# Three early output stores split by rows: 112 rows over sixteen DMA engines, and twice 8 rows over the lowest eight

## The chip, the core and the metric

The kernel runs on one core of one Trainium2 chip. The metric is device time in microseconds (us) of one execution. A core has five instruction streams: TensorE (PE, with its weight loads shown apart as PEld), VectorE (DVE), ScalarE (ACT), GpSimd (POOL) and SyncE (SP). It also has sixteen DMA engines, which move everything between the chip's memory (HBM) and the on-chip buffer SBUF (128 partitions), whichever stream asks for it. A DMA is asked for in one instruction; it is then carried out as packets, here one packet for each partition's row.

## The reference

Four batches; q, k and v are 4 x 6400 x 256 in fp32, and the result is 25600 x 256 in fp32.

```python
qn = q / (norm(q, axis=1) + 1e-6);  kn = k / (norm(k, axis=1) + 1e-6)
s = kn.transpose(0, 2, 1) @ qn / tau            # 256 x 256 for each batch
a = softmax(s, axis=-1)
x = (v @ a).reshape(25600, 256)
logits = x @ w_gate                              # 8 experts, the best 2 are kept
w = softmax of the two kept logits
out = x + sum over the two experts e of  w_e * ((x @ A[e]) @ B[e])     # A: 256 x 16, B: 16 x 256
```

## The kernel before

The 6400 rows of a batch are laid out as 128 partitions of 50 chunks: partition p holds rows 50p to 50p+49. A chunk is thus 128 rows of 256 numbers. q and k of a batch come in three tiles of 17, 17 and 16 chunks (`QK`), v and the result in five tiles of 10 chunks (`V`, `PC`). All tiles of q, k and v are loaded by DMAs that POOL asks for (`do_load`, L561) and that turn fp32 into bf16 on the way; the first four chunks of q and k of batch 0 come as fp32 by SP and ACT. The result goes out in fp32 by DMAs that SP asks for (`do_store`, L926). A full store is one tile of 10 chunks: 128 rows of 10,240 bytes, 1,280 KB. The last two tiles of the last batch go out as three smaller stores each, of 4, 4 and 2 chunks (`FINE`, `UNITS`).

For a batch, the G steps (L587) multiply k by q over the 50 chunks into PSUM, and norms are taken beside it. Then a short chain of small steps (L648 to L765) makes the softmax and the small matrices for gate and experts. For each v tile then: transposes (L788), gate (L812, L826, L835), experts' inner product (L879), their transposes (L902), and the output matmuls Y (L915, L920), whose PSUM results ACT or DVE copies into a y tile (L769, L771). There are seven y tiles (`STORE["y"]`), so that finished results can wait in SBUF.

The order of all steps is fixed before the program is built: `make_plan` lists the steps with a cost, an engine and a rank, and `Plan.run` plays them through once as a simulated schedule. Each engine's instructions are then written out in that order. POOL asks for the loads in the order of `WORDS`, as far as tiles are free. SP carries the stores in the order of the plan. `HOLD` (L409) keeps some early stores back behind a named load: SP first asks for a 16-element DMA out of that load's last row into `scrap` (L645), which can only be asked for once the load has landed, and the stores queue behind it. In the order that SP has them, the first stores (batch, tile) are: (0,2); a hold on k (1,2); (0,1); (0,3); a hold on k (3,1); (0,0); (1,0); a hold on k (3,2); and then the rest, from (2,0) to (3,4). The constant tables `PARTS`, `FINE`, `FIRST`, `OFF` and `MERGED` (L413 to L423) hold other choices of the schedule.

The plan itself knows a store only as one step (`"store", b, i, c, n`) with a size; how many DMAs `do_store` asks for is not seen there.

Of the kernel before, what the change touches and what calls it, by code (L numbers as in the profile page):

```python
# [32 lines left out]
class Clock:  # L33


    WINDOW, FIRST, LOW, HIGH = 3.413, 0.31, 0.5, 0.8

# [3 lines left out]
    def at(self, t):  # L41
        w = max(0, int((t - self.FIRST) / self.WINDOW) + 1)
        while len(self.cold) <= w:
            share = self.busy[-1] / self.WINDOW
            self.cold.append(share < (self.HIGH if self.cold[-1] else self.LOW))
            self.busy.append(0.0)
        return w

    def took(self, t, us):

        end, w = t, self.at(t)
        while us > 1e-9:
            pace = 2.0 if self.cold[w] else 1.0
            step = min(us * pace, max(self.FIRST + w * self.WINDOW - end, 1e-6))
            self.busy[w] += step
# [5 lines left out]
    def idle(self, t):  # L61

        w = self.at(t)
        return t - self.FIRST - (w - 1) * self.WINDOW - self.busy[w] > self.SPARE

# [165 lines left out]
def make_plan(B, order, ahead):  # L231
# [150 lines left out]
    for b in range(B):  # L382
        for i in range(NP):
            x = pos["v", b, max(g for g, (i0, _) in enumerate(V) if i0 <= i)]
            parts = UNITS if b == B - 1 and i >= NP - FINE else ((0, PC),)
            for c, n in parts:
# [25 lines left out]

PARTS = {(0, 0): ((0, 2), (2, 15)), (0, 2): ((34, 8), (42, 8)), (3, 2): ((34, 8), (42, 8))}  # L413
FINE = 2
FIRST = 4
OFF = {(0, 0, 'k'), (0, 0, 'q'), (0, 1, 'q'), (0, 2, 'k'), (0, 2, 'q'), (0, 4, 'q'), (0, 5, 'q'),
        (0, 6, 'k'), (0, 6, 'q'), (0, 7, 'k'), (0, 8, 'q'), (1, 0, 'k'), (1, 0, 'q'), (1, 1, 'q'),
# [41 lines left out]
def kernel(  # L459
# [11 lines left out]
    nc = tc.nc  # L471

    B, N, C = q.shape
    P = 128
# [15 lines left out]
    out_v = out.rearrange("(b p c) d -> b p c d", b=B, p=P)  # L490
# [44 lines left out]
    held = {}  # L535
# [25 lines left out]
    def do_load(s, what, b, i, c, n):  # L561
        if what == "v":
            t, src, c0 = sb(s, "v", (b, i), [P, PC * max(n for _, n in V), C], BF16), v_v, c
        else:
            t = sb(s, "qk", (what, b, i), [P, max(n for _, n in QK), C], BF16)
            src, c0 = {"q": q_v, "k": k_v}[what], QK[i][0]
            if (b, c) == (0, 0):
                n = FIRST
                if "first" not in W:
# [6 lines left out]
        if (what, b, i) in (("q", 0, 0), ("k", 0, 0)):  # L576
            c, n = FIRST, c + n - FIRST
        nc.gpsimd.dma_start(t[:, c - c0:c - c0 + n, :], src[b, :, c:c + n, :])  # L578
# [346 lines left out]

    def do_store(s, b, i, c, n):  # L926
        lo = i * PC + c
        nc.sync.dma_start(out_v[b, :, lo:lo + n, :], held["y", (b, i), ""][:, c:c + n, :])


    do = dict(load=do_load, wts=do_wts, sq=do_sq, add=do_add, red=do_red, n2p=do_n2p, hold=do_hold, warm=do_warm, cast=do_cast, G=do_G, accs=do_accs, n2=do_n2, rsqrt=do_rsqrt, rq_ps=do_rq_ps, s=do_s,
              exp=do_exp, recip=do_recip, aT_ps=do_aT_ps, aT=do_aT, waA_ps=do_waA_ps, waA=do_waA,
              a=do_a, ZL=do_ZL, ZLe=do_ZLe, T=do_T, Te=do_Te, log=do_log, loge=do_loge, Z=do_Z, Ze=do_Ze, gzT=do_gzT,
              gzTe=do_gzTe, Y=do_Y, Ye=do_Ye, store=do_store)
    for name in ("m1", "eq1", "lm", "m2", "mask", "msum", "t", "th", "g2"):
        do[name] = gate_step(name)
# [50 lines left out]
```

## Time and profile before

| | us |
|---|---|
| median of 7 runs | 254.31 (254.15 to 254.48) |
| the profiled execution | 254.56 |
| its span, first to last instruction | 252.8 |
| PE / DVE / ACT / POOL busy in the span | 218.7 / 192.6 / 151.1 / 27.0 |
| first full store asked for | 76.72 |
| last store asked for | 247.5 |

The DMAs' part: 11,243 packets, 66.70 MB counted at the written side, 78.91 MB read from HBM and 26.21 MB written to it. The DMA queues are numbered: q0 carries what POOL asks for, q1 what SP asks for, q10 what ACT asks for, q8 and q14 the fetches of the engines' own instructions.

How it is read: a profile is one execution; busy time of an engine is the sum of its instructions, and a "share" of DMA is the time of the packets over sixteen engines times the span. The profile holds start, duration, queue and size of each DMA packet and, for each DMA, sixteen times at which a part of it landed. It does not hold the number of the DMA engine.

### The profile page before, as it was taken

What the parts mean: (1) busy time and instruction counts of PE and PEld (TensorE: products, weight loads), DVE (VectorE), ACT (ScalarE), POOL (GpSimd) and SP (SyncE); (2) the same over time, 40 slices, a digit from 0 to 9 for tenths busy, and PEclk for the clock granted to TensorE, in tenths of its full rate; (3) what the DMA queues carried; (4) which work ended last, traced back from release to release, by engine and by line L of the source; (5) the groups of instructions that cost most, each with busy time, mean ns of one, the idle gap of its engine ahead of it and who ended that gap; (6) DMA issues with size and microseconds to landing.
All of it is one profiled execution on the core that took longest, in us unless ns stands there. A gap on an engine that the chain in (4) does not pass through costs nothing.

```text
span 252.8 us, 5852 instructions
## 1 busy us (share of the span) xinstructions
PE 218.7 (87%) x2357; PEld 193.7 (77%) x2357; DVE 192.6 (76%) x528; ACT 151.1 (60%) x269; POOL 27.0 (11%) x54
## 2 busy tenths in 40 slices
PE   0274997988999998689999999889999979999990
PEld 0152983876999996579899899779999769999980
DVE  0055589879898987588899899489898898889840
ACT  5354437556786543975667768362674846657671
POOL 7003110040002002000500100500000000000000
PEclk9999897999999999999999999999999999999997
DMA  8999999999999999999999999999999999999996
GB/s 246 215 216 212 214 220 212 212 220 216 216 215 246 304 304 295 225 216 219 212 212 219 217 216 217 212 211 317 316 251 352 324 336 321 340 385 426 398 408 243
DMA packets 11243, 66.70 MB, mean 264 GB/s; under 512 B 1360, under 2 KB 1744, under 8 KB 6608
## 3 DMA queue, kind: packets, MB, share of 16 engines
q0 software_dynamic: 6912, 38.80, 74.4%
q1 hardware_dynamic: 3968, 26.87, 26.2%
q10 hardware_dynamic: 336, 0.66, 0.8%
q8 instruction: 18, 0.29, 0.4%
q14 instruction: 9, 0.07, 0.1%
HBM read 78.91 MB, written 26.21 MB: 416 GB/s over the span
## 4 chain that ended last, share of the span: by engine, by line
PE 53%; DMA 32%; issue 5%; DVE 4%; ACT 3%; POOL 1%; POOLq 0%; DVEq 0%
DMA v<-in_v_dram 18%; PE Y_ps L915 13%; PE acc L593 10%; DMA qk<-in_q_dram 10%; PE Y_ps L920 6%; PE T_ps L788 5%; PE ZL_ps L812 5%; DMA qk<-in_k_dram 5%; PE gzT_ps L902 4%; PE acc L597 3%; PE acc L602 2%; PE Z_ps L879 1%; ACT a_exp L715 1%; DVE a_bf L763 1%; PE log_ps L826 1%
## 5 line engine op out<-in xcount | busy, mean ns | idle before, releaser
L593 PE MATMUL acc<-qk 128*128 128x256 bf16 x400 | 69.4, 281 | 17.1 <-DMA qk<-in_k_dram 9.6
L915 PE MATMUL Y_ps<-a_bf,vT 128*128 128x256 bf16 x400 | 60.0, 272 | 0.2 <-DVE acc_sb L710 0.2
L621 DVE TENSOR_TENSOR ssq<-ssq,sq 128x1280 f32<-128x1280 f32 (+1 forms) x27 | 43.3, 1605 | 20.0 <-ACT sq L615 19.9
L769 ACT COPY y<-Y_ps 128x512 f32<-128x512 f32 x79 | 46.2, 586 | 16.5 <-PE Y_ps L920 13.5
L593 PEld LDWEIGHTS <-qk 128*128 128x128 bf16 x400 | 34.3, 101 | 20.3 <-DMA qk<-in_k_dram 11.0
L615 ACT ACTIVATE sq<-qk 128x1280 f32<-128x1280 bf16 (+1 forms) x27 | 36.9, 1367 | 17.7 <-DVE ssq L621 16.6
L915 PEld LDWEIGHTS <-vT 128*128 128x128 bf16 x400 | 39.0, 98 | 4.6 <-issue 0.3
L920 PE MATMUL Y_ps<-ball,gzT 128*128 128x256 bf16 x200 | 38.2, 273 | 0.0
L597 PE MATMUL acc<-qk 128*128 128x128 bf16 x242 | 34.4, 224 | 0.0
L788 PE MATMUL T_ps<-ident,v 128*128 128x128 f32 x200 | 27.5, 274 | 0.6 <-DVE waA_sb L757 0.4
L769 ACT COPY vT<-T_ps 128x512 f32<-128x512 f32 (+1 forms) x44 | 21.2, 510 | 11.1 <-PE T_ps L788 10.7
L597 PEld LDWEIGHTS <-qk 128*128 128x128 bf16 x242 | 24.3, 100 | 3.5
L890 DVE TENSOR_TENSOR gz<-zl,gateg 128x256 bf16<-128x256 f32 x70 | 26.3, 443 | 0.3
L578 POOL DMA_DIRECT2D v<-in_v_dram x20 | 11.5, 575 | 133.5 <-PE T_ps L788 119.7
L788 PEld LDWEIGHTS T_ps<-ident,v 128*128 128x128 f32 x200 | 22.3, 141 | 1.6 <-DVE waA_sb L757 0.6
L602 PE MATMUL acc<-qk 128*128 128x128 bf16 x168 | 23.4, 222 | 0.0
L902 PE MATMUL gzT_ps<-ident,gz 128*128 128x128 f32 x100 | 20.9, 281 | 2.6 <-DVE gateg L868 1.4
L920 PEld LDWEIGHTS <-gzT 128*128 128x128 bf16 x200 | 19.6, 98 | 2.3
L812 PE MATMUL ZL_ps<-waA_sb,vT 128*128 128x136 bf16 x280 | 19.5, 223 | 1.7 <-DVE waA_sb L757 1.5
L771 DVE COPY gzT<-gzT_ps 128x256 f32<-128x256 f32 (+1 forms) x40 | 15.0, 379 | 7.2 <-PE gzT_ps L902 5.6
L812 PEld LDWEIGHTS <-vT 128*128 128x128 bf16 x280 | 17.7, 98 | 2.4 <-issue 2.1
L615 ACT ACTIVATE ssq<-qk 128x1536 f32<-128x1536 bf16 x8 | 11.9, 1487 | 11.8 <-DMA qk<-in_q_dram 7.7
(80 smaller groups left out, 273.3 us busy)
## 6 DMA issues: line engine op xcount, KB each, us to landing
out_dram<-y SPq DMA_DIRECT2D x18, 1280.0 KB, 16.6
v<-in_v_dram POOLq DMA_DIRECT2D x20, 640.0 KB, 20.3
qk<-in_q_dram POOLq DMA_DIRECT2D x7, 1088.0 KB, 23.5
qk<-in_k_dram POOLq DMA_DIRECT2D x7, 1088.0 KB, 28.2
qk<-in_q_dram POOLq DMA_DIRECT2D x4, 512.0 KB, 19.4
qk<-in_k_dram POOLq DMA_DIRECT2D x4, 512.0 KB, 22.8
qk<-in_q_dram POOLq DMA_DIRECT2D x2, 1024.0 KB, 19.4
qk<-in_k_dram POOLq DMA_DIRECT2D x2, 1024.0 KB, 23.7
```

What stands on the lines that cost most here:

```text
L593: nc.tensor.matmul(acc[ic][:, 0:256], kt[:, j, ic::CC], qt[:, j, :], start=c == 0, stop=False, skip_group_check=True)
L597: nc.tensor.matmul(acc[ic][:, 256:384], kt[:, j, ic::CC], kt[:, j, ic::CC], start=False, stop=False, skip_group_check=True)
L602: nc.tensor.matmul(acc[ic][:, 384:512], qt[:, j, ic * P:(ic + 1) * P], qt[:, j, ic * P:(ic + 1) * P], start=False, stop=c == NC - 1, skip_ ...
L615: nc.scalar.activation(out[:, 0:n, :], t[:, j:j + n, :], ACT.Square)
L621: nc.vector.tensor_tensor(out=t, in0=t, in1=held["sq", (w, b, g), ""][:, 0:n, :], op=OP.add)
L769: nc.scalar.copy(out, in_)
L788: nc.tensor.matmul(ps[:, j, :], vt[:, c + j, :].bitcast(FP32), W["ident32"], is_transpose=True, start=(j == 0), stop=(j == n - 1))
L812: nc.tensor.matmul(ps[:, j, :], vT_of(b, i, c + j)[:, :, ic], st[b]["waA"][:, ic, :], start=(j == 0 and ic == 0), stop=(j == n - 1 and ic ...
L890: nc.vector.tensor_tensor(out=pairs[:, h].rearrange("p c (e r) -> p c e r", e=E), in0=z[:, 2 * h:2 * h + 2, :].rearrange("p c (e r) -> p c ...
L902: nc.tensor.matmul(ps[:, j, :], pairs[:, j * P:(j + 1) * P], W["ident32"], is_transpose=True, start=(j == 0), stop=(j == n // 2 - 1))
L915: nc.tensor.matmul(ps[:, j, :], vT_of(b, i, c + j)[:, :, ic], st[b]["a"][:, ic, :], start=(j == 0 and ic == 0), stop=False, skip_group_che ...
L920: nc.tensor.matmul(ps[:, j, :], pair[:, :, j], W["B"], start=False, stop=(j == 1), skip_group_check=True)
```

## The change

`do_store` looks the tile (batch, tile) up in a new table, `SPLIT`. For three tiles, (0,2), (0,3) and (0,0), it asks for three DMAs in place of one: partitions 0 to 111, then 112 to 119, then 120 to 127, all with the same columns. The other stores are asked for as before, as one DMA of 128 partitions. The plan, the order of the steps, the loads and the computation stay as they are.

```diff
 FINE = 2
+SPLIT = {(0, 2): ((0, 112), (112, 8), (120, 8)), (0, 3): ((0, 112), (112, 8), (120, 8)), (0, 0): ((0, 112), (112, 8), (120, 8))}
 FIRST = 4
...
     def do_store(s, b, i, c, n):
         lo = i * PC + c
-        nc.sync.dma_start(out_v[b, :, lo:lo + n, :], held["y", (b, i), ""][:, c:c + n, :])
+        for p, rows in SPLIT.get((b, i), ((0, P),)):
+            nc.sync.dma_start(out_v[b, p:p + rows, lo:lo + n, :], held["y", (b, i), ""][p:p + rows, c:c + n, :])
```

A DMA of 112 rows is divided over sixteen engines as seven rows each, and one of 8 rows over the lowest-numbered eight engines as one row each. For the three tiles together, the lowest eight engines so carry 27 rows each in place of 24, and the highest eight 21.

## The prediction

> **What bounds the kernel now.** I began with the head of the page, because a change to stores can only matter where DMA does.
>
> ```profile
> span 252.8 us, 5852 instructions
> PE 218.7 (87%) x2357; PEld 193.7 (77%) x2357; DVE 192.6 (76%) x528; ACT 151.1 (60%) x269; POOL 27.0 (11%) x54
> DMA  8999999999999999999999999999999999999996
> q0 software_dynamic: 6912, 38.80, 74.4%
> q1 hardware_dynamic: 3968, 26.87, 26.2%
> q10 hardware_dynamic: 336, 0.66, 0.8%
> q8 instruction: 18, 0.29, 0.4%
> q14 instruction: 9, 0.07, 0.1%
> ```
>
> PE is busy for 87%, but the DMA row has a 9 in every slice but the first and the last, and the shares of the queues add up to 74.4 + 26.2 + 0.8 + 0.4 + 0.1 = 101.9% of sixteen engines' span (a packet starts some ns before the one ahead of it ends, so over 100 is possible). The second view, busy time by stretches, shows where there is room at all. Its columns are the stretch, its length, busy time of PE, PEld, DVE, ACT and POOL, granted clock, DMA share, GB/s.
>
> ```profile
> 106.00:166.00 60.00, 57.82 (x629) 52.74 (x627) 51.28 (x134) 40.97 (x74) 8.46 (x16) 1.00 1.04 215
> 226.00:238.00 12.00, 12.00 (x150) 11.32 (x149) 10.98 (x37) 8.18 (x19) 0.00 (x0) 1.00 1.01 423
> 238.00:240.00 2.00, 2.00 (x26) 1.89 (x25) 1.65 (x5) 0.93 (x4) 0.00 (x0) 1.00 0.83 342
> 240.00:248.00 8.00, 6.83 (x61) 5.79 (x59) 3.26 (x10) 5.92 (x11) 0.00 (x0) 1.00 1.00 407
> 248.00:252.80 4.80, 0.00 (x0) 0.00 (x0) 0.00 (x0) 0.00 (x0) 0.00 (x0) 0.65 0.48 191
> ```
>
> The DMA engines are full until 238, some of them rest between 238 and 240, and after 248 only DMAs run. So an engine's end is the sum of its own packets, and the kernel's end is that of the slowest engine. The chain of waits names PE for 53%, as it runs back from the last store through the matmuls. But the last store is asked for at 247.47, its first part lands at 249.98, and its last at 252.05: the end is decided by those 2.07 us between DMA engines.
>
> The third view is the trace's packets and landings. All rows are dealt evenly, so why do engines differ? The sixteen landings of a store in the stretch of stores (asked for at 219.65) and of the last store:
>
> ```
> 219.65: 232.81 232.91 233.06 233.07 233.56 233.59 233.89 | 235.01 235.08 235.20 235.30 235.31 235.41 235.53 235.72 236.53
> 247.47: 249.98 249.99 250.01 250.03 250.06 250.15 250.23 | 250.51 250.64 250.74 250.84 250.97 251.16 251.17 251.88 252.05
> ```
>
> Seven engines are early and nine late. A packet follows the one before it on its engine at a fixed offset, so I chained the packets into sixteen tracks by their ends and by the order that each queue gives an engine. (Where two tracks pass within some ns they can be exchanged; I know of such places near 170 and 240.) The 18 q8 packets, 16 KB of instructions each, take 0.95 us on average (17.1 in all), and the engine that has one falls back by that much. They go to only eight tracks, in a fixed rotation: 30.6, 48.8, 59.1, 72.1, 84.1, 94.0, 111.9, 122.4, and again in that order from 134.0 and from 226.8. So two engines carry three blocks and six carry two. These eight are among the late nine, and the two with three are those that land last. The ninth late track holds five q14 packets (8 KB, 0.31 to 0.32 us and slower neighbours; 50.6, 103.5, 157.9, 201.7, 246.0). These come at the pace of DVE's instructions. I put its last landing at 251.16.
>
> The Trainium skill ("Runtime: NRT & Kernel Launch", Instruction fetch mechanics) says that instructions stream in blocks of 16 KiB and that crossing a boundary is mostly hidden. The size agrees; hidden it is for PE, but not for the DMA engine, which is held for 0.95 us. By the rule alone all engines would end together, and moving rows to eight of them could only delay the end.
>
> **The change part by part.**
>
> *Rows moved.* A 10,240-byte packet of a store takes 0.394 us from start to next start beside loads, and 0.381 when only stores run. The three stores lie beside loads. Each of the lowest eight engines gets 27 rows for 24: +3 x 0.394 = +1.18 us. Each of the highest eight gets 21: -1.18. Neither is lost on the way, as no engine rests before 238.
>
> *Extra ends.* Each DMA ends with a packet of 4 bytes on each engine it uses, some 0.01 us: six more on the lowest eight, +0.06.
>
> *Extra issues.* SP issues six more DMAs at 0.333 to 0.366 us each.
>
> ```profile
> 76.72 0.37 SPq L928 DMA_DIRECT2D out_dram<-y  x1
> 77.83 0.60 SPq L645 DMA_DIRECT2D scrap<-qk  x1
> 78.48 0.56 SPq L928 DMA_DIRECT2D out_dram<-y  x1
> 89.82 0.33 SPq L928 DMA_DIRECT2D out_dram<-y  x1
> 166.95 0.51 SPq L645 DMA_DIRECT2D scrap<-qk  x1
> 167.51 1.05 SPq L928 DMA_DIRECT2D out_dram<-y  x2
> ```
>
> Behind (0,2) at 76.72 the hold is queued. It goes out at 77.83, after its load has landed at 77.81; 0.37 + 2 x 0.33 us puts SP at 77.75, still before it. Behind (0,3) at 89.82 nothing is issued until 166.95. Behind (0,0) stands (1,0), 0.67 us later, but its packets wait in the ring for some 6 us behind those of (0,0) anyway. So nothing; without this cover it would be 0.67 us at one place. The y tiles come free after three landings in place of one; the last of them is up to 1.2 us later on a lowest engine. Seven tiles cover this. If they did not, PE would lose 1.2 us at most, and PE has the 2.5 us from the last issue to the first landing behind a DMA end that is later still.
>
> *The price of a row in the new form.* The trace has no store of 8 or 112 rows. Below, a row costs what it costs now (0.394). Above, the nearest row is a store packet just behind an instruction block, which reads up to 0.767, +0.37. As for many engines on few partitions, in the first us sixteen engines write 512-byte rows into 32 partitions and hold 0.027 us a packet until 4.7; later they slow to 0.05, together with the other queue's packets. That row is the nearest in kind, and up to 4.7 it shows no toll. I take 0 and keep up to +0.37 for each of the six single rows (2.2 us on the lowest eight).
>
> The Trainium skill speaks against the new form: "SBUF — State Buffer" (Door 1: The DMA port swizzle) has 112 to 127 on four of sixteen ports, and "DMA: Bandwidth & Descriptors" (Rules for kernel authors) advises one transfer of 128 partitions over two for halves. By it, four engines reading one port would take 4 x 0.385 = 1.54 us where each row now takes 0.385. No run here shows it.
>
> *The sum.* What matters is which tracks are the lowest eight; the trace gives no numbers. If the eight with the blocks are the upper half, the two worst go from 252.05 and 251.88 to 250.87 and 250.70, a relief of 1.18. But the lower half then holds the seven early tracks and the ninth late one. The early ones have 1.1 us of rest at 238 to 240 and 1.8 us at the end, so +1.24 costs nothing there. The ninth goes from 251.16 to 251.16 + 1.24 = 252.40: it becomes the last, and the end moves by 252.40 - 252.05 = +0.35. On the profiled 254.56 that is 254.91; the profiled execution is 0.25 above the median, so on the median it is 254.66, and as the late tracks beside the ninth end a little earlier, I say 254.6. Three rows are more than the balance asks for: with one row the last would be 251.66.
>
> **The rivals.**
>
> *A, above: traded.* The relieved eight give up 1.18, the engine of DVE's instructions takes over: 254.6. If its track is taken wrongly by one place (neighbours 250.5 to 251.17), the end lies between 251.75 and 252.41, thus 254.0 to 254.7; with some toll 254.9.
>
> *B, the wrong half.* If the blocks go to the lowest eight, or to a mix that holds one with three, that one gets all: 252.05 + 1.24, +1.24 us: 255.55. It decides as soon as one of the two three-block tracks has a number below eight. For it: nothing in the trace ties a rotation of eight to the upper half. Against it: nothing either. Where a store or load meets empty rings, block tracks start 0.1 us later on average in the four loads after 191, which would suit higher numbers, but the spread of single starts is 0.4 or more.
>
> *C, the toll.* Single rows out of 8 neighbouring partitions, or seven rows out of blocks not aligned as before, are slower. With half of the bound, 6 x 0.185 = 1.1 on the lowest eight, and 0.02 for each of the 21 other rows, 0.4: +0.35 + 1.5, about 256.1. It decides from a toll of 0.03 us a single row on, the point at which 254.8 is passed. Against it stand the 512-byte rows, for it that all 128-row stores share rows out in one way, and these not.
>
> *D, relief that lasts.* If the ninth late track is not among the lowest eight, the end falls to the next of the late ones: 252.05 - 1.18 = 250.87, -1.18, or some of that: 253.6 as a middle. Against it: eight block tracks leave no room in the upper half for a ninth.
>
> *E, not as said.* If the 8 rows go to other engines each time, or to sixteen, the shift is spread thin, and 254.3 stays.
>
> **How the numbers follow.** Chances: A 0.43, B 0.22, C 0.17, D 0.12, E 0.06. A measurement of this kernel can tell about 0.2% from no change, 0.5 us. Below 253.8: most of D, and a little of A for a track taken wrongly, 0.13. Between 253.8 and 254.8: A's larger part, E, the rest of D, 0.43. Above 254.8: B, C, and 0.05 of A, 0.44. The likeliest is A at 254.6, within 254.0 to 254.9 for itself. The range is 253.6 (the middle of D) to 256.1 (the middle of C); it leaves out half of D and half of C.
>
> **What would show it.** Right: the sixteen landings of the last store no longer fall into seven and nine with two stragglers; the two three-block tracks end 1.2 us earlier against the early seven, and one track with 8 KB blocks ends last, near 252.4; store packets of 10,240 bytes keep 0.39 us; SP's hold still goes out at 77.8. B is right if the three-block tracks lie 1.2 us further out. C shows in store packets of 0.5 us and more between 80 and 105. D shows in a last landing below 251.7. Wrong altogether would be a DMA row with slices under 9, an end that follows PE's last matmul, or a shift of the tail by something other than some multiple of a row's 0.39 us.

## The result, and the profile after

| | before | with the change |
|---|---|---|
| median (range), us | 254.35 (254.15 to 254.54) | 255.34 (254.73 to 255.91) |
| ratio | | 1.0039, 95% interval 1.0031 to 1.0047 |
| profiled execution, its span | 254.56, 252.8 | 255.13, 253.3 |
| last store asked for, last landing | 247.47, 252.05 | 247.13, 252.47 |
| span's end minus last landing (span not rounded) | 0.74 | 0.84 |

The change costs 0.99 us (0.79 to 1.20); the forecast was 254.6, +0.3, so its sign was right and its size a third. The range of single runs is three times as wide as before, 1.18 us against 0.39.

The head of the page of the changed kernel:

```profile
span 253.3 us, 5864 instructions
PE 219.5 (87%) x2357; PEld 194.0 (77%) x2357; DVE 192.7 (76%) x528; ACT 151.2 (60%) x269; POOL 27.0 (11%) x54
DMA  8999999999999999999999999999999999999995
q0 software_dynamic: 6912, 38.80, 74.2%
q1 hardware_dynamic: 4016, 26.87, 26.2%
q10 hardware_dynamic: 336, 0.66, 0.8%
q8 instruction: 18, 0.29, 0.4%
q14 instruction: 9, 0.07, 0.1%
```

Bytes, shares and busy times are those of before; only q1 has 4016 packets for 3968, the 48 extra ends (six DMAs of 8 rows, eight engines each), which is what the edit says. The busy time by stretches (stretch, length, busy time of PE, PEld, DVE, ACT and POOL, granted clock, DMA share, GB/s):

```profile
106.00:166.00 60.00, 57.83 (x630) 52.76 (x627) 51.28 (x134) 40.80 (x74) 8.46 (x16) 1.00 1.03 215
238.00:240.00 2.00, 2.00 (x27) 1.86 (x25) 2.00 (x6) 0.93 (x3) 0.00 (x0) 1.00 0.90 374
240.00:248.00 8.00, 6.48 (x58) 5.46 (x56) 2.91 (x9) 5.57 (x11) 0.00 (x0) 1.00 1.00 411
248.00:253.30 5.30, 0.00 (x0) 0.00 (x0) 0.00 (x0) 0.00 (x0) 0.00 (x0) 0.66 0.42 169
```

Between 238 and 240 the engines are busy for 0.90 in place of 0.83. That does not show that rows have filled the early tracks' rest: the kernel before with two small DMAs, in which no row moves (below), has 0.93 there. After 248 still only DMAs run, so it is still the slowest DMA engine that ends the kernel. SP's queue in order of time (start, length, instruction, count):

```profile
76.94 1.08 SPq L930 DMA_DIRECT2D out_dram<-y  x3
78.12 0.59 SPq L646 DMA_DIRECT2D scrap<-qk  x1
167.55 0.52 SPq L646 DMA_DIRECT2D scrap<-qk  x1
168.11 1.78 SPq L930 DMA_DIRECT2D out_dram<-y  x4
```

The three issues of (0,2) take 1.08 us, and the hold goes out at 78.12. Its load landed at 77.83 in this execution, 0.29 us earlier; in the kernel before, the hold followed its load by 0.02 (77.83 and 77.81). The next load's hold, at 167.55, stands 0.6 behind that of before, and no slice of the DMA row falls below 9 for it. The landings of the last store:

```
before   249.98 249.99 250.01 250.03 250.06 250.15 250.23 250.51 250.64 250.74 250.84 250.97 251.16 251.17 251.88 252.05
after    249.68 249.69 249.71 249.72 249.76 249.80 250.02 250.10 250.65 250.93 251.03 251.07 251.12 251.81 251.82 252.47
```

I chained the packets into sixteen tracks again; now the 8-row DMAs name the half of each track, and the first two split stores give their single rows to the same eight tracks. Between the halves, these two stores make a difference of 1.58 us = 4 x 0.394 (two rows more on one side, two fewer on the other). The track with DVE's 8 KB blocks is among the lowest eight and ends last, at 252.47. Of PE's eight block tracks, six are in the upper half, the two with three blocks among them; the third and the fourth of the rotation (blocks at 60.1 and 72.0) are in the lower half, and end at 251.81 and 251.82. Of the 48 single-row packets 44 take 385 to 398 ns; four are slow, in two pairs that overlap in time: 668 and 888 ns at 87.2, 1086 and 752 ns at 177.8 and 178.05. Overlap alone does not make a row slow: of the first 8-row DMA, seven single rows run at one moment (starts 85.76 to 86.12) at 385 to 398 ns each.

### The profile page after: what moved, and what is told of

The parts are those of the page before. It is cut to its first block, busy times and chain, and to the rows that moved or that the text cites. A ratio compares the mean times of both kernels' runs of the same rounds, so it can differ in the third digit from the quotient of the medians.

```text
span 253.3 us, 5864 instructions
## 1 busy us (share of the span) xinstructions
PE 219.5 (87%) x2357; PEld 194.0 (77%) x2357; DVE 192.7 (76%) x528; ACT 151.2 (60%) x269; POOL 27.0 (11%) x54
## 3 DMA queue, kind: packets, MB, share of 16 engines
q1 hardware_dynamic: 4016, 26.87, 26.2%
## 4 chain that ended last, share of the span: by engine, by line
PE 45%; DMA 40%; issue 6%; DVE 3%; ACT 2%; POOL 1%; POOLq 0%; DVEq 0%
DMA v<-in_v_dram 18%; DMA qk<-in_k_dram 13%; PE Y_ps L916 12%; DMA qk<-in_q_dram 9%; PE acc L594 7%; PE Y_ps L921 6%; PE T_ps L789 5%; PE ZL_ps L813 4%; PE gzT_ps L903 4%; PE acc L598 2%; PE acc L603 1%; PE Z_ps L880 1%; POOL qk L579 1%; ACT a_exp L716 1%; PE log_ps L827 1%
```

## The experiments

Theory A is the balance of rows: an end is worth 0.394 us times the rows moved, and DVE's track takes over. The rivals are a toll on rows in the new form, and, after the first four kernels, a third thing that was not on my list: the end of the program. All times are medians in us; each set of kernels ran beside the kernel before, which is 254.35 to 254.43 in every set, and kernels of different sets are compared through it. The landings and the last column come from one profiled execution of each kernel.

| kernel | DMAs more | median (range) | ratio to before, 95% interval | last landing | from there to the span's end |
|---|---|---|---|---|---|
| one split | 2 | 254.50 (254.30 to 255.08) | 1.0006, 0.9997 to 1.0015 | 251.63 | 1.09 |
| two splits | 4 | 254.74 (254.55 to 255.09) | 1.0016, 1.0007 to 1.0025 | 251.80 | 0.97 |
| 16 rows in place of 8 + 8 | 3 | 254.70 (254.56 to 254.83) | 1.0012, 1.0003 to 1.0021 | 251.92 | 1.04 |
| six splits | 12 | 257.40 (256.89 to 257.63) | 1.0116, 1.0102 to 1.0130 | 254.20 | 0.96 |
| one split, six small DMAs | 8 | 254.03 (253.95 to 254.63) | 0.9990, 0.9981 to 0.9998 | 251.43 | 0.72 |
| before, two small DMAs | 2 | 254.77 (254.57 to 255.10) | 1.0016, 1.0007 to 1.0025 | 251.80 | 1.10 |
| the change, two small DMAs | 8 | 255.18 (254.71 to 255.61) | 1.0038, 1.0025 to 1.0052 | 252.20 | 0.74 |
| extra rows, neighbours | 6 | 256.30 (256.20 to 256.47) | 1.0078, 1.0065 to 1.0090 | 253.84 | 0.84 |
| extra rows, spread | 6 | 256.27 (256.03 to 257.13) | 1.0083, 1.0067 to 1.0098 | 253.36 | 0.86 |
| the change again | 6 | 255.06 (254.95 to 255.82) | 1.0034, 1.0022 to 1.0047 | 252.64 | 0.84 |
| five DMAs, neighbours | 16 | 255.46 (255.36 to 256.07) | 1.0044, 1.0030 to 1.0057 | 253.53 | 0.74 |
| five DMAs, spread | 16 | 254.85 (254.71 to 255.40) | 1.0018, 1.0009 to 1.0026 | 252.16 | 0.73 |

### How many rows

One split store, (0,2) alone:

```diff
-SPLIT = {(0, 2): ..., (0, 3): ..., (0, 0): ...}
+SPLIT = {(0, 2): ((0, 112), (112, 8), (120, 8))}
```

> Only the store (0,2) is split. Balance of rows (each split gives the lowest eight engines one row more, +0.41 us with its ends, and takes 0.39 us from the upper eight; nothing else): the two tracks with three 16 KB blocks go from 252.05 to 251.66, the track with DVE's instruction blocks from 251.16 to 251.57, so the end moves by -0.39 us: about 253.95 us. Toll (single rows out of eight neighbouring partitions are held up, which made the difference between 0.35 and the measured 0.99 us with three splits, so 0.2 us a split): about 254.15 us, with one or two single rows of 0.6 us or more between 86 and 89.

Two, (0,2) and (0,3):

> The stores (0,2) and (0,3) are split, (0,0) is not. Balance of rows: DVE's track ends at 251.16 + 0.82 = 251.98, the three-block tracks at 251.26: -0.07 us, 254.3 us, no change that can be told. Toll of 0.2 us a split on top of it: 254.7 us. If the time is as with three splits, the third split costs nothing and the reason lies in the first two.

Six, (0,1), (1,0) and (2,0) beside the three:

> The first six stores are split, (0,2), (0,1), (0,3), (0,0), (1,0), (2,0). Balance of rows: DVE's track takes six rows, 251.16 + 6 x 0.41 = 253.62: +1.57 us, 255.9 us. Toll of 0.2 us a split beside it: another 1.2 us, 257.1 us. If early engines' rest near 239 could take the rows in, the time would stay near that of three splits.

With one row moved the last landing is at 251.63, where the balance had 251.66, and yet the kernel is not faster: 254.50, above both expectations (253.95 and 254.15), with no slow single row in its profile. With two it is 251.80 (balance 251.98), and the kernel is 0.38 slower; that is the time that the toll was expected to give, but this profile has no slow single row either. So the landings follow the balance, and the time does not follow the landings. With six the last landing is 0.6 past the balance, and store packets are slow: between 193.9 and 198.7 twenty of them take 0.65 us or more, the worst 1527 ns. The last split store, (2,0), has only sixteen single rows, so ordinary rows are among these. The DMA row of that page shows for the first time a slice under 9 between the first and the last (near 240):

```profile
span 255.2 us, 5873 instructions
DMA  8999999999999999999999999999999999999894
```

### The form without the rows

```diff
+SPLIT = {x: ((0, 112), (112, 16)) for x in ((0, 2), (0, 3), (0, 0))}
```

> The same three stores as 112 rows and one DMA of 16 rows, which goes to all sixteen engines: every engine keeps its 24 rows, and nothing is moved between them. Balance of rows: only three ends of 0.01 us are added: 254.4 us, no change. Toll: 16 single rows a store instead of 16 on eight engines, so as many single rows in all, now on the late tracks of the upper half as well: 0.3 to 0.9 us, 254.7 to 255.3 us, with single rows of 0.6 us or more. If the form with 112 rows alone costs time (engines no longer read the same partitions as before), it shows here too, in packets of the 112 rows.

The last 16 rows of the same tiles go to sixteen engines, one row each, so nothing moves between halves. None of the 48 single rows is slow and the last landing, 251.92, is 0.13 earlier than in the profile before; the kernel is 0.34 slower all the same. Neither a toll nor the balance explains that; what is left is the time after the last landing, 1.04 us in place of 0.74.

### The end of the program

The trace has SP's waits at the very end, after its last store: one instruction for each pair of semaphores, in a fixed order of numbers. Each DMA of SP and ACT is given one of eight semaphores in turn. From the records of SP (start of the instruction, the DMA semaphore that it waits for, and the last landing of that kernel):

```
before      111 at 248.98   116 at 250.22   117 at 251.43   118 at 252.07                     (landing 252.05)
one split   107 at 251.02   108 at 251.64   109 at 251.71   110 at 251.77   111 at 251.83
            116 at 251.89   117 at 251.95   118 at 252.01                                     (landing 251.63)
```

Before, SP and ACT ask for 32 DMAs, four full turns, so the last store is on 118, which is waited for last: 0.02 us after the landing this wait is over, and only the program's last few instructions follow. With two more, the last store is on 108, and six waits of 0.06 us still follow, though all they wait for has landed: +0.37. With three it is five waits, with four or twelve it is four, with six (the change) two, +0.12. The time from the last landing to the end goes in these steps in all fourteen profiles: 0.72 to 0.74 with no wait behind, 0.84 to 0.86 with two, 0.96 to 0.97 with four, 1.04 with five, 1.09 to 1.10 with six. To test it, small DMAs of 4 bytes, asked for while SP is idle near the start, turn the semaphores on:

```diff
+        for x in range(6):
+            nc.sync.dma_start(pad[:, x:x + 1], moe_w_gate[0:1, x:x + 1])
...
+    pad = nc.dram_tensor("pad_words", (1, 8), FP32, kind="Internal").ap()
```

> One split store (0,2), and six DMAs of 4 bytes each at the start (from HBM to a spare tensor in HBM), so that the number of DMAs of SP and ACT grows by eight, one full rotation of the eight semaphores, in place of two. Theory 'balance and end waits': the last landing stays at 251.6 to 251.8 as with one split alone, the last store is again on the semaphore that SP waits for last, and the 0.37 us of six more waits are gone: 0.75 us from last landing to end of span in place of 1.07, median 254.0 (253.9 to 254.15). Rival 'the end waits cost nothing' (the last landing is not what ends the kernel): 254.5 as with one split alone.

> No split at all; two DMAs of 4 bytes at the start, from HBM to a spare tensor in HBM. No row of a store moves and no form of a store changes. Theory 'end waits': the last store goes to the second of the eight semaphores that SP waits for at the end, six more waits of 0.06 us follow the last landing: +0.37 us, 254.7 (254.6 to 254.8), with the last landing still at 252.05. Rival 'the end waits cost nothing': 254.35.

> The change whole, and two DMAs of 4 bytes at the start (from HBM to a spare tensor in HBM): eight more DMAs than before, so the last store is on the last semaphore again. Theory 'balance and end waits': last landing 252.4 to 252.6, tail 0.75, so 0.12 us less than the change alone: 255.2. Theory 'toll by chance': single-row packets of over 0.6 us again, at other places and in another number than in the profile of the change (4 of 48), and the range of the runs over 0.8 us wide; median 255.0 to 255.4. Rival 'toll by place': the same two pairs are slow, near 87 and 178.

All three times came out as the end waits have it; the last landings came out 0.17 to 0.25 earlier than expected. The kernel before, with two such DMAs and nothing else, is 0.39 slower (254.77; from its last landing to the end 1.10 in place of 0.74). One split with a full turn is 254.03, 0.47 under the same split without it. Its page and its issues of SP (the second fence: what is written, how many, KB each):

```profile
span 252.2 us, 5863 instructions
DMA  8999999999999999999999999999999999999996
q1 hardware_dynamic: 3996, 26.87, 26.2%
```

```profile
out_dram<-y SPq DMA_DIRECT2D x2, 80.0 KB
pad_words<-in_moe_w_gate_dram SPq DMA_DIRECT2D x6, 0.0 KB
```

In packets the six DMAs cost twelve of 4 bytes (3996 = 3968 + 16 ends + 12 of the small DMAs), and the span is 0.5 us shorter than with one split alone (252.7). This is the one version that is faster than the kernel before, by 0.35 us between the medians; the ratio's interval, 0.9981 to 0.9998, stops just short of 1. The kernel before with eight small DMAs, a full turn without any split, was not run. The change itself with a full turn is 255.18, 0.16 less than without, which is within the width of its runs. Its slow single rows came back near 178 (702, 1012 and 753 ns), not near 87.

### The price of a row

Six extra rows on the lowest eight engines, taken off no one, from neighbouring partitions or from partitions that lie 16 apart:

```diff
+        for x in range(2 if (b, i) in SPLIT else 0):
+            nc.sync.dma_start(spare[SPLIT.index((b, i)), x], held["y", (b, i), ""][slice(112 + 8 * x, 120 + 8 * x), c:c + n, :])
```

and for the spread copy `slice(7 + 8 * x, P, 16)`.

> All stores as before, and behind each of the stores (0,2), (0,3) and (0,0) two more DMAs of 8 rows each, from partitions 112 to 119 and 120 to 127, into a spare tensor in HBM (extra work, no part of the result). The lowest eight engines get six rows more, the upper eight give none up; six more DMAs, so the end waits are those of the change. Theory 'balance': the lowest engine with a late track goes from 251.16 by 6 x 0.394 + 0.06 to 253.6; span 254.4, 256.1 us median (255.8 to 256.4), and the copy with spread partitions the same. Theory 'toll by neighbouring partitions': single-row packets of 0.6 us and more here, 256.5 and over, and over 0.3 us more than the copy with spread partitions.

> The same as the copy with neighbouring partitions, but the two more DMAs of 8 rows take partitions 7, 23, 39 ... 119 and 15, 31, 47 ... 127, so that the eight rows of one DMA lie 16 partitions apart. Theory 'balance': 256.1 us (255.8 to 256.4), as with neighbours. Theory 'toll by neighbouring partitions': no single-row packet over 0.5 us, 256.1, while the copy with neighbours is over 0.3 us slower. Theory 'toll of the single row as such' (a DMA with one row an engine, wherever it lies): slow single packets here too, and no difference between the two copies.

> The change once more, word for word, for a second profile and a second set of runs beside the copies. Theory 'toll by place': single-row packets of (0,0) near 177.8 are slow a third time (752 to 1086 ns so far); those near 87 may be or not. Theory 'toll by chance': slow ones elsewhere or none. Median 255.2 to 255.5 by both, range over 0.8 us wide.

Both copies are at 256.3, 0.2 above the balance's 256.1: the arithmetic of rows holds over six rows as it did over one. The copy with neighbours has two slow single rows (972 and 871 ns at 179.7), the spread one has none; the medians show no difference. The change run again is at 255.06, below the 255.2 to 255.5 expected, with slow rows at 86.5 (1095 and 569 ns) and again near 179 (621, 1035 and 741 ns). So slow rows stand near 178 in all three profiles of the change, and near 87 in two of them.

That left open whether slow rows cost the change anything, so the last pair puts the question to the change's own rows. Each of the three stores goes out as five DMAs, 64, 32, 16, 8 and 8 rows; in one copy the partitions of a DMA are neighbours, in the other they lie 2, 4, 8 and 16 apart. Sixteen more DMAs (four of them small) make two full turns.

```diff
+ROWS = (slice(0, 128, 2), slice(1, 128, 4), slice(3, 128, 8), slice(7, 128, 16), slice(15, 128, 16))
+SPLIT = {(0, 2): ROWS, (0, 3): ROWS, (0, 0): ROWS}
...
-        nc.sync.dma_start(out_v[b, :, lo:lo + n, :], held["y", (b, i), ""][:, c:c + n, :])
+        for r in SPLIT.get((b, i), (slice(0, P),)):
+            nc.sync.dma_start(out_v[b, r, lo:lo + n, :], held["y", (b, i), ""][r, c:c + n, :])
```

The copy with neighbours has `slice(0, 64), slice(64, 96), slice(96, 112), slice(112, 120), slice(120, 128)`.

> The same three stores, each as five DMAs of neighbouring partitions: 64, 32 and 16 rows (four, two and one row on each of sixteen engines), and twice 8 rows as in the change. The same rows move to the lowest eight as in the change. With four DMAs of 4 bytes at the start there are sixteen more DMAs than before, two full rotations, so the tail after the last landing is 0.75 us. Theory 'balance': as the change with two such DMAs, 255.2, and 0.1 for the extra ends: 255.3 (255.0 to 255.5). Theory 'toll of neighbouring partitions': slow single-row packets (over 0.6 us) here, more than the four or so in the change, as sixteen rows more are single: 255.4 to 255.9.

> The same as the copy with neighbouring partitions, but the five DMAs take every second partition, then every fourth, eighth and twice every sixteenth of the rest: the rows that engines read at one time lie apart. Theory 'balance': 255.3, no difference between the two copies. Theory 'toll of neighbouring partitions': no slow single rows, a narrow range of the runs, and 0.2 to 0.5 us under the copy: 254.9 to 255.0, which is what the balance alone gives from the landings of an undisturbed kernel before (DVE's track at 251.2 + 1.24 = 252.44 against 251.8: +0.64 on 254.35).

255.46 against 254.85: rows that lie apart save 0.61 us, and the two intervals (1.0030 to 1.0057 and 1.0009 to 1.0026) do not meet. All five DMAs are spread in that copy, not the single rows alone. With neighbours two single rows are slow, 981 ns at 178.3 and 1180 ns at 178.8, fewer than expected; with spread rows none is, but the range of its runs is no narrower (0.69 us against 0.71). The last stretch of the two (neighbours first):

```profile
248.00:254.30 6.30, 0.00 (x0) 0.00 (x0) 0.00 (x0) 0.00 (x0) 0.00 (x0) 0.50 0.33 134
```

```profile
248.00:252.90 4.90, 0.00 (x0) 0.00 (x0) 0.00 (x0) 0.00 (x0) 0.00 (x0) 0.56 0.41 162
```

Both have nearly the same work left at 248: 6.30 x 0.33 = 2.08 and 4.90 x 0.41 = 2.01 us an engine, alike within the rounding of the shares. Yet the first ends 1.4 us later: its landings are all in by 251.88 but for one, at 253.53. So the delay sits on one engine. The slow packets explain only part of it: they overlap in time, so they lie on two engines, and one engine lost at most 0.79 us (1180 over 394 ns). The profiles also show the extremes: of the neighbours one of the two slowest of five runs (256.07), of the spread rows the fastest of eleven (254.71).

## Why the prediction was right and wrong

**The bound: right.** DMA stays full to 238, nothing but DMA runs after 248, and the last landing moves with the rows: 251.63, 251.80, 252.47 and 254.20 for one, two, three and six. (Without a split it was 252.05 in one execution and 251.80 in another, so 0.2 between two of them tells little.)

**Rows moved, 3 x 0.394: right.** 1.58 between the halves after two stores; one row gave 251.63 for 251.66, six extra rows 256.3 for 256.1.

**Who is last: right, with one detail wrong.** "If the eight with the blocks are the upper half" holds for six of the eight. The two that are not did not matter: they had two blocks, and end 0.65 before DVE's track. Case A names the track and its end, 252.40 for 252.47. The nearest to a case where only rows decide is the spread copy with five DMAs: +0.42 (254.85 - 254.43), for +0.35 predicted. One small step in that sum was loose: I took the 0.25 by which the profiled execution lies above the median off all tracks alike. In the kernel before with two small DMAs the last three landings are 251.20, 251.79 and 251.80, so in that execution the surplus is gone from the three-block tracks alone, and the sum on the median would have been 251.20 + 1.24 - 251.80 = +0.64. The 0.42 lies between the two.

**The toll, taken as 0: the step that failed.** I let the 512-byte rows at 0.027 us stand for it, because they were the nearest in kind. They are small loads into 32 partitions, and say nothing about rows of 10 KB read out of 8. The pair of five DMAs puts a price on neighbouring partitions, 0.61 with 96 single rows; the change has 48. (The extra copies, with 48 single rows, put it at nothing: 256.30 and 256.27.) For the change itself the toll is only what is left over: 0.99 - 0.12 - 0.42 leaves 0.45, the change with a full turn of semaphores 255.18 - 254.38 - 0.42 some 0.4, the second set of runs 255.06 - 254.35 - 0.12 - 0.42 leaves 0.2. With 0.64 for the balance in place of 0.42 it would be 0.2 or nothing, so its size stays open. Case C had the toll, but in another form: not 0.03 us or more on every row, but three to five rows in 48 that lose 0.2 to 0.7 us each. Such a row can cost the kernel only where it falls on an engine that ends late; whether that made the range of the runs wide is not shown, as kernels without slow rows in their profile have wide ranges too (0.78 with one split, 1.10 for the spread extra rows). The Trainium skill ("SBUF — State Buffer", Door 1: The DMA port swizzle) had been weighed in the prediction as an estimate of 1.54 us a row. The pair of five DMAs agrees with its direction, since spreading the rows helps there; the extra copies do not show it. No run agrees with its size: 44 of 48 rows here took 385 to 398 ns, and in the kernel with 112 + 16 rows sixteen engines read partitions 112 to 127 for one DMA and none of the 48 rows was slow.

**Extra issues, "nothing": half right.** The three issues took 1.08 us where the prediction had 1.03, and the hold, which was to go out with its load still ahead of it, went out 0.29 us behind the load (0.20 when the change was run again); no slice of the DMA row shows a gap for it. But more DMAs do cost something, at the other end of the program: 0.12 us in the change, up to 0.37 in its parts. The prediction counted what an added DMA issues and missed what it adds to the waits behind it, though the trace of before has these waits. So the measured 0.71 to 0.99 is +0.42 for the balance, +0.12 for the end, and a rest of 0.2 to 0.45, which is put down to slow rows.

**The rivals.** B (the wrong half) is out: by the tracks both three-block tracks are in the upper half, and no landing is near B's 253.29 (252.05 + 1.24). The measured 255.34 is nearest to B's 255.55 all the same, and A by itself reached only 254.9: that the result lies in the stated range is owed to the room left for B and C, so in part to luck. D (relief that lasts) is out, as DVE's track is in the lower half. With one row the relief does last, but by A's balance: one split with a full turn is 254.03, the 0.4 that the prediction gave in passing (251.66). E is out, as the same eight tracks took the single rows of both early split stores.

**What stays open.** Why the store (0,0), near 178 to 180, had slow rows in all five profiles with these three tiles and 8-row DMAs of neighbours, while sixteen rows at the same place had none and six splits had one of 564 ns there; why the extra copies differ in slow rows and not in the median; and what the rest of the 1.4 us between the two copies of five DMAs is. The change's own three DMAs with spread rows were not tried.

## What to carry to other kernels

When only DMA is left at the end, list the last landings engine by engine: a row moved from a late engine to an early one is worth its packet time, but the latest engine on the receiving side limits how much can be moved, and here one row was the whole of it. If rows go to a few engines, try partitions that lie apart: one pair of kernels here gained 0.61 us by it, another nothing. And look at what still waits behind the last landing: here a gain of 0.4 us was lost because the number of added DMAs was not a multiple of eight, the number of semaphores that SP and ACT take in turn.

## What the runs showed that I had not expected

- The end of this program costs 0.06 us for each pair of semaphores that SP still has to wait for after the last landing, even if both have been met. Two 4-byte DMAs at the start, which move nothing of use, made the kernel 0.39 us slower; six of them made the kernel with one split 0.47 faster.
- Slow single-row packets come in groups that overlap in time (1086 with 752 ns, 1095 with 569, 981 with 1180). Whether these packets slow each other is not shown; most others of the same DMA pass at 385 to 398 ns.
- By the tracks, PE's instruction blocks rotate over eight engines that are neither the upper nor the lower half (six and two), and DVE's five blocks go to one engine, in the lower half.
